# RWKV attention and a token mixer in one kernel: V in its loaded rows, scores by token parity, the bonus summed in PSUM

## The chip, the cores and the metric

The kernel runs on one core of a Trainium2 chip. The metric is device time in microseconds (us), the median of several runs. Five units take part: TensorE (PE) multiplies and writes only to PSUM, the accumulator memory; VectorE (DVE) and ScalarE (ACT) do elementwise work and are the ones that carry results out of PSUM; GpSimd (POOL) works between SBUF tensors here; SyncE (SP) issues the DMA transfers.

## The reference

Shapes: batch B = 4, heads H = 8, tokens S = 768, head width D = 48; the model width is H x D = 384.

```python
for t in range(S):
    cur = einsum('bhd,bhe->bhde', u * k[t], v[t])
    y[t] = einsum('bhd,bhde->bhe', r[t], state + cur)
    state = w[t][..., None] * state + einsum('bhd,bhe->bhde', k[t], v[t])
x = y.transpose(0, 2, 1, 3).reshape(B, S, 384)
wq, wk = x @ w_q, x @ w_k                        # 384 -> 64
W = einsum('bsd,btd->bst', wq, wk) / 8           # tokens by tokens, no softmax
out = maximum(einsum('bst,btd->bsd', W, x), 0) @ w_out
```

The first part is a linear recurrence with a decay w for each channel and token, and a bonus u for the current token. The second mixes all 768 tokens of a batch. All inputs and outputs are float32 in HBM.

## The kernel before

**Units.** The work is cut into 12 units, three of 256 tokens for each batch. A unit is two chunks of 128 tokens, called c = 0 and 1. A load puts two neighbouring tokens of all heads into one partition: partitions 0 to 63 hold chunk 0, the others chunk 1, and j = 0 or 1 is the token's parity. From unit 1 on, k and r are loaded with four tokens to a partition row (`load_long`, L237), and the V of the last batch is loaded at once in four scattered pieces (`load_whole`, L243).

**The recurrence as matrix products.** For each unit ScalarE takes the logarithm of w (`ln`, tile lw). TensorE sums the logarithms over the tokens with a triangle of ones (`cw`), and ScalarE turns the sums into `ep` (exponential) and `en` (exponential of the negative). A constant MU is added to each logarithm ("centring", SHIFT), and the factors gx, gv, gk, US and IDU take it out again. TensorE transposes k and r (`kT`, `rT`) with a permutation PM, so that channels lie on partitions. Elementwise products then give RT = r ep (step `RT`, L516), KT = k en (`KT`, L521 and L526) and qT = r k for the bonus (`qT`, L506); `ks` is a copy of the turned k in SBUF.

- Scores: `A` multiplies KT by RT for each head and chunk, 128 tokens by 128, and `AM` (L595) multiplies by the causal mask US on VectorE.
- V: `v16` casts it to bf16, `vp` multiplies by PM to bring its rows into the chunk order, and `VB` copies that out of PSUM.
- State: `kb` turns KT back, `kd` copies it out with the factor gk, `sn` multiplies it by VB and adds the old state through IDU, and `SB` multiplies by the decay.
- Output: `yi` is RT times the old state and `ya` is AM times VB, both summed in PSUM in tile y. The even and odd heads lie in separate banks of y, except in the last unit.
- Bonus: `dps` sums qT times u, `dd` copies the sums out, `Vd` (L575) multiplies them by VB on GpSimd, and `X` (L710, L715) computes y gx + Vd on VectorE, into X in bf16.

**The mixer.** `xt` and `XT` turn X, `qk` gives both projections, `QK` copies them out. After the third unit of a batch, `T` sums wk times X over all tokens, `TS` copies it out, and for each unit `mx`, `rl` (relu), `fp` (times w_out), `os` (copy) and `st` (store) finish.

**What sets the order.** Nothing is scheduled at run time. `add` collects steps with their key, the engines they may run on, and what they come after. WAYS picks an engine for each step that has a choice (E or e or c TensorE, D or d VectorE, A ScalarE, P GpSimd), BANKS places the PSUM tiles in the eight banks, and ORDER is the written order in which all steps are issued. Each engine runs its own steps strictly in that order and waits by semaphores. `RINGS` says how many buffers each tile has: four for the loaded tensors, two for most others. All transfers but two of u and one store are issued on SP's queue in its order. The steps `z` are products of zeros that keep TensorE busy.

The instructions of TensorE all carry the line of the helper `mm`, L179; the copies those of `copy`, L327 to L335.

```python
s["eng"] = self.ENGINE[s["way"]]
...
for i in ORDER:
    s = self.steps[i]
    assert all(x["out"] for x in s["after"]), s["key"]
```

Of the kernel before, what the change touches and what calls it, by code (L numbers as in the profile page):

```python
# [12 lines left out]
I32 = mybir.dt.int32  # L13
# [10 lines left out]
class Buf:  # L24
    def __init__(self, kind, tile=None):
        self.kind = kind
        self.tile = tile
        self.filler = None
        self.before = None
        self.bank = None  # L30


class Plan:

    ENGINE = dict(E="E", e="E", c="E", A="A", D="D", d="D", P="P", S="S", Q="Q", L="L")
# [5 lines left out]
    def add(self, key, ways, fn, after=(), buf=None, reads=(), cols=0, mode=0, behind=None,  # L43
            half=-1, more=None):
        s = dict(key=key, ways=ways, way=ways[0], fn=fn, after=list(after), buf=buf,
                 reads=list(reads), cols=cols, mode=mode, behind=behind, half=half,
                 more=more or {}, i=len(self.steps), fills=False, out=False)
        if buf is not None:
            if buf.filler is None:
                buf.filler = s  # L50
                s["fills"] = True
                if buf.tile is None:
                    self.banks.append(buf)
                elif behind is None and buf.before is not None:
                    s["behind"] = buf.before.filler
            elif behind is None:
                s["behind"] = buf.filler
        self.steps.append(s)
        return s

    def order(self):
        ways = iter(WAYS)
        for s in self.steps:
            if len(s["ways"]) > 1:
                s["way"] = next(ways)
                assert s["way"] in s["ways"], s["key"]
            s["eng"] = self.ENGINE[s["way"]]
        for b, x in zip(self.banks, BANKS):
            b.bank = x
        assert sorted(ORDER) == list(range(len(self.steps)))  # L70
        done = []
        for i in ORDER:
            s = self.steps[i]
            assert all(x["out"] for x in s["after"]), s["key"]
            if s["buf"] is not None and s["buf"].kind == "x":
                s["buf"].kind = "s" if s["way"] == "E" else "w"
            s["out"] = True
            done.append(s)
        return done


ORDER = [
# [40 lines left out]
]  # L123
WAYS = (
    "PDDDAPPDDdPADPPDDEEEAAPPAdPAAPEAcEEAAPPAPPADPeDEEDAAAAAAAAPPDPDADPeAcEEDAPPAdPAAPEAEEEDA"
    "PPDPPAAPeAEEAAAAAAAAAAPDPPAAPEDEcEAAPPDPPDAPEAEEEAAPPDPPAAPeDceAAAAADADDPAAPPAPEDcEEDAPP"
    "DPPAPeAcceAAPPDPPPAPPAEEDDAEDADAAADAAAADADDA"
)
BANKS = [
# [9 lines left out]
WARM = 12  # L139
# [3 lines left out]
def kernel(  # L143
# [27 lines left out]
    LONG = tuple(range(1, N))  # L171
    WHOLE = (B - 1,)

    SHIFT = 25
    MU = -SHIFT * math.log(2.0) / C
    UNIT = 2.0 ** -SHIFT

# [9 lines left out]
    def const(shape, dtype, name):  # L187
# [3 lines left out]
    EW = 136  # L191
    KW = 64 + 16 * 128
# [5 lines left out]
        kd=(2, KW, BF16), lw=(2, 1024, BF16), r16=(2, 1024, BF16), k16=(2, 1024, BF16),  # L198
        ep=(2, 8 * EW, BF16), en=(2, 1024, BF16), ks=(2, 1024, BF16), qT=(2, 1024, BF16),
        RT=(2, 1024, BF16), KT=(2, 1024, BF16), v16=(2, 2 * DM, BF16), VB=(2, 2 * DM, BF16),  # L200
        dd=(2, 2 * H, F32), Vd=(2, 2 * DM, BF16), AM0=(2, 1024, BF16), AM1=(2, 1024, BF16),
        SB=(4, NP * D, BF16), XT=(2, 2 * DM, BF16), MX=(4, 2 * DM, BF16), X=(2, NCH * DM, BF16),
        QK=(2, QW, BF16), TS=(2, DM, BF16), vw=(2, NCH * DM, F32))
    if not WHOLE:
        del RINGS["vw"]
# [14 lines left out]
    PM = const([C, C], BF16, "PM")  # L220
    IDU = const([C, C], BF16, "IDU")
    Z = const([C, 512], BF16, "Z")
    US = const([C, C], F32, "US")
# [24 lines left out]
    def setup():  # L248
        pads = [[64, 16], [1, 16]]
        nc.vector.memset(Z, 0.0)  # L250
        for _ in range(18):
            mm(PS[:, ds(0, 512)], Z[:, ds(0, C)], Z)
# [641 lines left out]
```

## Time and profile before

| | |
|---|---|
| time, median of 3 runs | 102.12 us (101.38 to 103.38) |
| the profiled execution's own time | 101.37 us |
| its span | 99.6 us |
| PE busy | 86.6 us, 1906 matmuls |
| VectorE busy | 84.9 us, 154 instructions |
| ScalarE busy | 79.0 us, 135 instructions |
| GpSimd busy | 69.5 us, 82 instructions |
| HBM read, written | 19.66 MB, 4.72 MB |
| granted TensorE clock | 1.0 |

The profile is of one execution. The span goes from its first to its last instruction. A group's row gives the busy time of its instructions together, the mean of one in ns, and the idle time of the engine just before them with what ended it. In a timeline, a row is a run of like instructions: its start, how long it lasted, and how many. Neighbouring instructions of one engine overlap somewhat, and a matmul's end is modelled, so the distance from one start to the next says more than the length. PE's busy time counts overlapping matmuls once.

### The profile page before, as it was taken

The page shows a single profiled execution, that of the slowest core. Times are in us where ns is not written, and L with a number is a line of the kernel's source. Part 1 is how long each engine was busy: PE and PEld are TensorE (multiplying, and loading weights), DVE is VectorE, ACT ScalarE, POOL GpSimd, SP SyncE. Part 2 cuts the span into 40 slices and gives each one's busy share as a digit, 9 for nine tenths or more (in the row PEclk, how much of TensorE's full clock was granted, in tenths as well). Part 3 has the DMA queues.
Part 4 walks back from the last instruction along what each step waited for, and adds up shares of the span by engine and source line. Part 5 has one row for each costly group of instructions (what it writes and reads, how often), then busy time and mean ns, then how long its engine had stood idle before and what let it go on. Part 6 is the DMA issues. An engine that isn't in the chain of part 4 may idle for free.

```text
span 99.6 us, 4492 instructions
## 1 busy us (share of the span) xinstructions
PE 86.6 (87%) x1906; PEld 63.3 (64%) x1911; DVE 84.9 (85%) x154; ACT 79.0 (79%) x135; POOL 69.5 (70%) x82
## 2 busy tenths in 40 slices
PE   5978796879886998999999999889998999999930
PEld 1325473756774767777776777759787687776610
DVE  6284999799979999979999999999999799783740
ACT  6034998799996799899999998999899766666920
POOL 6866354999799895799999989498996392500000
PEclk9999999999999999999999999999999999999999
DMA  1999999799999999999999977998993056030794
GB/s 17 313 327 349 324 337 296 195 295 335 289 314 298 225 311 329 344 321 268 271 330 305 316 114 218 251 156 201 282 417 115 7 210 264 10 158 7 277 367 149
DMA packets 45141, 24.68 MB, mean 248 GB/s; under 512 B 31552, under 2 KB 43968, under 8 KB 45120
## 3 DMA queue, kind: packets, MB, share of 16 engines
q1 hardware_dynamic: 44960, 24.19, 84.0%
q8 instruction: 15, 0.25, 0.9%
q10 hardware_dynamic: 160, 0.20, 0.5%
q14 instruction: 6, 0.05, 0.1%
HBM read 19.66 MB, written 4.72 MB: 245 GB/s over the span
## 4 chain that ended last, share of the span: by engine, by line
PE 37%; DVE 23%; SPq 20%; DMA 7%; issue 7%; ACT 3%; ACTq 0%; DVEq 0%
PE PS L179 37%; SPq L232 9%; SPq L237 8%; DMA vg<-in_v_dram 7%; DVE AM L595 7%; DVE X L710 6%; DVE RT L516 3%; SPq L355 2%; DVE qT L506 2%; DVE ks L333 2%; DVE SB L658 1%; ACT VB L327 1%; SPq L357 1%; ACT MX L339 1%; DVE kd L335 1%
## 5 line engine op out<-in xcount | busy, mean ns | idle before, releaser
L595 DVE TENSOR_TENSOR AM<-PS,US 128x1024 bf16<-128x1024 f32 x24 | 28.8, 1218 | 0.7 <-PE PS L179 0.7
L526 POOL TENSOR_TENSOR KT<-ks,en 128x1024 bf16<-128x1024 bf16 (+1 forms) x10 | 19.7, 1965 | 4.7 <-DVE ks L333 3.3
L575 POOL TENSOR_TENSOR Vd<-VB,dd 128x768 bf16<-128x768 bf16 (+1 forms) x14 | 18.1, 1293 | 4.5 <-ACT dd L327 3.4
L454 ACT ACTIVATE en<-PS 128x1024 bf16<-128x1024 f32 (+1 forms) x14 | 12.5, 907 | 3.0 <-PE PS L179 2.9
L179 PEld LDWEIGHTS <-KT 48*128 48x128 bf16 (+1 forms) x312 | 9.7, 94 | 6.6 <-issue 4.5
L447 ACT ACTIVATE ep<-PS 128x512 bf16<-128x512 f32 (+1 forms) x28 | 13.7, 555 | 0.1
L179 PE MATMUL PS<-wo,MX 128*128 128x384 bf16 x72 | 13.5, 327 | 0.0
L710 DVE SCALAR_TENSOR_TENSOR X<-PS,gx,Vd 128x384 bf16<-128x384 f32 x22 | 12.5, 609 | 0.7 <-PE PS L179 0.6
L407 ACT ACTIVATE lw<-wg 128x768 bf16<-128x768 f32 x12 | 10.3, 857 | 2.9 <-DMA wg<-in_w_dram 2.9
L179 PE MATMUL PS<-RT,KT 48*128 48x128 bf16 x192 | 9.7, 218 | 1.2 <-ACT VB L327 0.4
L327 ACT COPY os<-PS 128x768 f32<-128x768 f32 (+1 forms) x11 | 7.9, 714 | 3.5 <-PE PS L179 3.5
L418 POOL CAST k<-kg 128x768 bf16<-128x768 f32 x10 | 8.3, 827 | 2.5 <-DMA kg<-in_k_dram 2.5
L179 PE MATMUL PS<-Z 128*128 128x512 bf16 x25 | 8.4, 461 | 1.4 <-DVE Z L250 1.2
L418 POOL CAST r<-rg 128x768 bf16<-128x768 f32 x10 | 8.2, 825 | 1.6 <-DMA rg<-in_r_dram 1.6
L179 PEld LDWEIGHTS <-MX 128*128 128x128 bf16 x72 | 6.5, 97 | 3.6 <-DVE MX L341 0.2
L516 DVE TENSOR_TENSOR RT<-PS,ep 128x1024 bf16<-128x1024 bf16 (+1 forms) x14 | 8.4, 605 | 0.0
L179 PE MATMUL PS<-VB,AM 128*128 128x48 bf16 x192 | 8.0, 184 | 0.4 <-issue 0.4
L506 DVE TENSOR_TENSOR qT<-PS,ks 128x1024 bf16<-128x1024 bf16 x12 | 8.2, 684 | 0.1
L339 ACT ACTIVATE MX<-PS 128x768 bf16<-128x768 f32 (+1 forms) x12 | 8.0, 682 | 0.4
L179 PE MATMUL PS<-CM,lw 64*128 64x128 bf16 x192 | 7.4, 217 | 0.5 <-DVE AM L595 0.3
L327 ACT CAST VB<-PS 128x768 bf16<-128x768 f32 x8 | 6.4, 804 | 1.1 <-PE PS L179 0.6
L179 PEld LDWEIGHTS <-AM 128*128 128x128 bf16 x192 | 6.3, 96 | 1.6 <-issue 0.7
(90 smaller groups left out, 191.9 us busy)
## 6 DMA issues: line engine op xcount, KB each, us to landing
kg<-in_k_dram SPq DMA_DIRECT2D x12, 384.0 KB, 6.4
wg<-in_w_dram SPq DMA_DIRECT2D x12, 384.0 KB, 5.0
rg<-in_r_dram SPq DMA_DIRECT2D x12, 384.0 KB, 5.8
vg<-in_v_dram SPq DMA_DIRECT2D x9, 384.0 KB, 6.3
out_dram<-os SPq DMA_DIRECT2D x9, 384.0 KB, 2.5
vw<-in_v_dram SPq DMA_DIRECT2D x4, 288.0 KB, 6.7
out_dram<-os SPq DMA_DIRECT2D x5, 192.0 KB, 2.4
wof<-in_moe_w_out_dram SPq DMA_DIRECT2D x1, 576.0 KB, 6.2
```

Source lines behind the costliest of these rows:

```text
L179: return nc.tensor.matmul(o, l, rr, start=start, stop=stop, skip_group_check=True, is_transpose=trans)
L327: nc.scalar.copy(o, i)
L407: nc.scalar.activation(view(lw.tile, 0, [[64, H], [512, 2], [1, D]]), view(g["wg"].tile, 0, [[D2, H], [D, 2], [1, D]]), ACT.Ln, bias=0.0, ...
L418: op(view(o.tile, 0, [[64, NP], [256, 4], [1, D]]), view(g[src].tile, 0, [[2 * D2, NP], [D, 4], [1, D]]))
L447: nc.scalar.activation(view(ep.tile, cs[0] * NP * EW + off, [[EW, NP * len(cs)], [step, 2], [1, 32]]), view(at(cw), cs[0] * 512 + j * 64, ...
L454: nc.scalar.activation(en.tile[:, ds(cs[0] * 512, w_)], at(cw)[:, ds(cs[0] * 512, w_)], ACT.Exp, bias=0.0, scale=-1.0)
L506: lambda e: nc.vector.tensor_tensor(plain(qT.tile), turned(512), plain(ks.tile), ALU.mult),
L516: nc.vector.tensor_tensor(plain(RT.tile, cs, 32), turned(512, cs, True), plain(ep.tile, cs, EW // 4), ALU.mult)
L526: x.tensor_tensor(KT.tile[:, cols], ks.tile[:, cols], en.tile[:, cols], ALU.mult)
L575: (nc.vector if e == "D" else nc.gpsimd).tensor_tensor(Vd.tile[:, cols], VB.tile[:, cols], view(dd.tile, cs[0] * H, [[1, len(cs) * H], [0, ...
L595: AMs[c] = add(("AM", n, c), "D", lambda e, c=c, A=A: nc.vector.tensor_tensor(view(AM[c].tile, 0, [[C, 8], [1, C]]), view(at(A), 0, [[C, 8 ...
L710: nc.vector.scalar_tensor_tensor(view(X.tile, 2 * i * DM + hh * D, [[D2, H], [1, D]]), view(at(y), hh * 512, [[D, H], [1, D]]), gx, view(V ...
```

## The change

- V stays in its loaded rows of two tokens: `vp` and `VB`, the permutation PM and `load_whole` go; `v16` (three buffers) is what all products read. k and r are loaded in two-token rows too; `load_long` goes.
- No centring: MU, gx, gv, gk, UNIT and IDU go. `kd` is a plain copy.
- Scores by the parity j of the key token, on tiles of 64 rows by 64 columns. A step `A` has 16 products in place of 8, and its mask is US[j]. `ya` sums over j and over chunk halves: 16 products of 64 rows in place of 8 of 128.
- State: `sp` is the products of kd and v16 on 64x64 tiles, `so` adds the old state through ID16.
- The bonus is added in PSUM: `yd` multiplies Vd by the identity into y, and `X` is a plain copy of y on ScalarE or VectorE.
- All heads of a chunk now lie in one bank of y. `yi` is in two steps, one for each pairing of chunk and half of the partitions. Where both kinds of rows would meet in y, order() sets a drain of TensorE before the step (20 places).
- `kb` and `xt` are always on tiles of 64 rows. `ep` is one activation in place of two, and `ep` and `RT` aren't halved in the first and last unit.
- New ORDER, WAYS and BANKS; 8 z steps in place of 12, 16 products of zeros at the start in place of 18. By the new WAYS, X runs on ScalarE but for one half, KT mostly on VectorE (GpSimd keeps 6 pieces of KT out of 10, and 10 of Vd out of 14), and XT, QK and dd more often on VectorE.

```diff
+            if s["rows"] is not None:
+                x, kind = s["rows"]
+                s["drain"] = x.rows.get(1 - kind) == drains
+                drains += s["drain"]
+                x.rows[kind] = drains
...
-    v16=(2, 2 * DM, BF16), VB=(2, 2 * DM, BF16), ... vw=(2, NCH * DM, F32)
+    v16=(3, 2 * DM, BF16)
...
+        def f_ep(e):
+            nc.scalar.activation(view(ep.tile, 66, [[EW, 8], [-65, 2], [1, 64]]),
+                                 view(at(cw), 0, [[C, 8], [64, 2], [1, 64]]), ACT.Exp)
...
             def f_A(e, j=j, A=A):
                 for hp in range(NP):
-                    for hh in range(2):
-                        mm(x[:, ds(hh * 512 + hp * C, C)],
-                           KT.tile[ds(hh * 64, D), ds((c * NP + hp) * C, C)],
-                           RT.tile[ds(hh * 64, D), ds((c * NP + hp) * C, C)])
+                    for c in range(2):
+                        for hh in range(2):
+                            mm(x[ds(c * 64, 64), ds(hh * 512 + hp * C, C)],
+                               KT.tile[ds(hh * 64, D), ds((2 * hp + j) * C + c * 64, 64)],
+                               RT.tile[ds(hh * 64, D), ds((c * NP + hp) * C, C)])
...
+                        for c in chunks:
+                            mm(at(sn[c])[ds(hh * 64, 64), ds(hp * D, D)],
+                               kd.tile[ds(c * 64, 64), ds((j * H + h) * 64, 64)],
+                               v16.tile[ds(c * 64, 64), ds(j * DM + h * D, D)],
+                               start=(j == 0 and hp == 0), stop=True)
...
+        for hx in range(2):
+            halves = [(c, c ^ hx) for c in range(2) if olds[c] is not None]
+            def f_yi(e, hx=hx, halves=halves):
+                for hp in range(NP):
+                    for c, hh in halves:
+                        mm(of(c, 2 * hp + hh), RT.tile[ds(hh * 64, D), ds((c * NP + hp) * C, C)],
+                           olds[c].tile[ds(hh * 64, D), ds(hp * D, D)],
+                           start=y.begin(c), stop=False)
...
+                    for c in range(2):
+                        mm(of(c, h), AM[j].tile[ds(c * 64, 64), ds((hh * NP + hp) * C, C)],
+                           v16.tile[ds(c * 64, 64), ds(j * DM + h * D, D)],
+                           start=y.begin(c), stop=True)
...
+        def f_yd(e):
+            first = [y.begin(c) for c in range(2)]
+            for j in range(2):
+                for c in range(2):
+                    mm(at(y)[ds(j * 64, 64), ds(c * 512, DM)], ID16[ds(c * 64, 64), ds(c * 64, 64)],
+                       Vd.tile[ds(c * 64, 64), ds(j * DM, DM)], start=first[c])
...
-                    nc.vector.scalar_tensor_tensor(
-                        view(X.tile, 2 * i * DM + hh * D, [[D2, H], [1, D]]),
-                        view(at(y), hh * 512, [[D, H], [1, D]]), gx,
-                        view(Vd.tile, hh * D, [[D2, H], [1, D]]), ALU.mult, ALU.add)
+            xs = add(("X", n, c0), "AD", lambda e, c0=c0, nc_=nc_: copy(
+                e, view(X.tile, (2 * i + c0) * DM, [[DM, nc_], [1, DM]]),
+                view(at(y), c0 * 512, [[512, nc_], [1, DM]])),
+                yss, [X], [(y, sum(1 << c for c in cs))], cols=DM * nc_)
...
         for s in plan.order():
+            if s["drain"]:
+                nc.tensor.drain()
```

More of the change, by code (lines that the diff above doesn't have):

```diff
@@ L41, in __init__, with add @@
         self.banks = []
[L43 to L57, printed above, removed]
+    def add(self, key, ways, fn, after=(), writes=(), reads=(), cols=0, mode=0, more=None,
+            rows=None):
+        full = lambda x: x if isinstance(x, tuple) else (x, 3)
+        s = dict(key=key, ways=ways, way=ways[0], fn=fn, after=list(after),
+                 writes=[full(x) for x in writes], reads=[full(x) for x in reads], cols=cols,
+                 mode=mode, more=more or {}, i=len(self.steps), out=False, drain=False, rows=rows)
+        for x, _ in s["writes"]:
+            if x.banks and x not in self.banks:
+                self.banks.append(x)
         self.steps.append(s)
@@ new lines, in spread @@
+        def spread(t, place, pitch, js):
+            if len(js) == 2:
+                return view(t, place, [[64, 8], [pitch, 2], [1, 64]])
+            return view(t, place + js[0] * 64, [[C, 4], [pitch, 2], [1, 64]])
+        ens, KTs = {}, {}
+        for js in fine:
+            x = add(("en", n, js[0]), "A", lambda e, js=js: nc.scalar.activation(
+                packed(en.tile, js), spread(at(cw), 0, 512, js), ACT.Exp, scale=-1.0),
+                [cws], [en], [cw], cols=512 * len(js))
+            for j in js:
+                ens[j] = x
@@ L562, in f_dps @@
             x = at(dps)
-            for c in range(2):
+            for j in range(2):
                 for hp in range(NP):
-                    mm(x[:, ds(c * H + hp * 2, 2)], qT.tile[:, ds((c * NP + hp) * C, C)],
-                       view(UB, hp, [[NP, 2]]), start=(c == 0 and hp == 0), stop=True)
-        dpss = add(("dps", n), "E", f_dps, [qTs, wts["u"]], dps, [qT])
+                    mm(x[:, ds(j * H + hp * 2, 2)], qT.tile[:, ds((2 * hp + j) * C, C)],
+                       view(UB, hp, [[NP, 2]]), start=(j == 0 and hp == 0), stop=True)
@@ L627, in unit @@
-        olds, oldss = [], []
-        for c in range(2):
-            old = batch.get("SB")
-            olds.append(old)
-            oldss.append(batch.get("SBs"))
-            if final and c == 1:
-                break
-            sn, SB = bank(), ring("SB")
-            def f_sn(e, c=c, old=old, sn=sn):
-                x = at(sn)
-                for o in range(2 if e == "c" else 1) if old is not None else ():
-                    rows = ds(o * 64, 64) if e == "c" else ds(0, 128)
-                    mm(x[rows, ds(0, NP * D)], IDU[:, rows], old.tile, start=True, stop=False)
+                    for c in range(2):
[3 more added lines that the diff above has]
+                               RT.tile[ds(hh * 64, D), ds((c * NP + hp) * C, C)])
@@ L641, in f_sn, with f_sp @@
+        chunks = [0] if final else [0, 1]
+        sn = [bank() for _ in chunks]
+        olds, oldss = [batch.get("SB")], [batch.get("SBs")]
+        def f_sp(e):
+            for j in range(2):
                 for hp in range(NP):
@@ L661, in unit @@
-                [sns, eps[c]], SB, [sn, ep])
-        ys = [bank(), bank()] if end else [wide()] * 2
-        yis, yas = {}, {}
-        def of(c, h):
-            return at(ys[c])[:, ds(h * D if end else h % 2 * 512 + (c * NP + h // 2) * D, D)]
-        def f_yi(e, c, start):
-            heads = [(hp, hh) for hp in range(NP) for hh in range(2)]
-            if end:
-                heads.sort(key=lambda x: x[1])
-            for x, (hp, hh) in enumerate(heads):
-                if end and x == NP:
-                    nc.tensor.drain()
-                mm(of(c, 2 * hp + hh), RT.tile[ds(hh * 64, D), ds((c * NP + hp) * C, C)],
-                   olds[c].tile[ds(hh * 64, D), ds(hp * D, D)],
-                   start=(start and hp == 0 and not (end and hh)), stop=False)
@@ L697, in unit @@
-        for c in range(2):
-            if c not in yas:
-                y_add(c)
+                ("SB", n, c), "D", lambda e, c=c, SB=SB: nc.vector.tensor_tensor(
+                    view(SB.tile, 0, [[D, NP], [1, D]]), view(at(sn[c]), 0, [[D, NP], [1, D]]),
+                    view(ep.tile, c * NP * EW + 64, [[EW, NP], [0, D]]), ALU.mult),
+                [x, eps], [SB], [sn[c], ep])
+            olds.append(SB)
+            oldss.append(batch["SBs"])
+        y = wide()
+        def of(c, h):
+            return at(y)[:, ds(c * 512 + h * D, D)]
```

472 lines of the change are left out of this document (163 added, 309 removed), and 92 rows, old and new, of tables (BANKS, ORDER).

## The prediction

> **What bounds the kernel now.** First the page: busy shares, the slices, the chain.
>
> ```profile
> span 99.6 us, 4492 instructions
> PE 86.6 (87%) x1906; PEld 63.3 (64%) x1911; DVE 84.9 (85%) x154; ACT 79.0 (79%) x135; POOL 69.5 (70%) x82
> ...
> PE   5978796879886998999999999889998999999930
> ...
> DVE  6284999799979999979999999999999799783740
> ...
> PE 37%; DVE 23%; SPq 20%; DMA 7%; issue 7%; ACT 3%; ACTq 0%; DVEq 0%
> ```
>
> The chain has three stretches: loads at first, VectorE in the middle, TensorE at the end. PE's digits overstate it, since a pipelined matmul counts until its modelled end, so I check with busy time by stretch and then with the timeline.
>
> ```profile
> 30.00:40.00 10.00, 8.70 (x235) 6.69 (x232) 10.00 (x17) 8.36 (x14) 8.39 (x8) 1.00 1.02 293
> ...
> 50.00:60.00 10.00, 9.64 (x233) 7.38 (x227) 10.00 (x17) 9.93 (x18) 9.46 (x9) 1.00 0.96 260
> 60.00:70.00 10.00, 9.42 (x276) 7.47 (x274) 10.00 (x17) 9.64 (x16) 8.24 (x7) 1.00 1.00 214
> ```
>
> After the length come the busy times of PE, weight loads, DVE, ACT and POOL; then the clock (full), the DMA share, GB/s. VectorE has no gap in 30 of these us, ScalarE hardly one. The loads run at 0.96 to 1.02 of the DMA engines, so they aren't idle either. VectorE's own timeline, first and last piece of its stretch:
>
> ```profile
> 8.52 0.69 DVE L333 COPY ks<-PS 128x1024 bf16<-128x1024 bf16 x1 [0.94 <-PE PS L179]
> ...
> 83.23 2.34 DVE L595 TENSOR_TENSOR AM<-PS,US 128x1024 bf16<-128x1024 f32 x2
> ```
>
> From 8.52 to 85.57 VectorE is paced by little but itself; after the last score mask AM, TensorE and the final token mixing take over. Two AM take 2.34, though one alone reads 1.218 below, so a VectorE instruction costs its mean less about 0.08; I use that throughout.
>
> ```profile
> L595 DVE TENSOR_TENSOR AM<-PS,US 128x1024 bf16<-128x1024 f32 x24 | 28.8, 1218 | 0.7 <-PE PS L179 0.7
> L710 DVE SCALAR_TENSOR_TENSOR X<-PS,gx,Vd 128x384 bf16<-128x384 f32 x22 | 12.5, 609 | 0.7 <-PE PS L179 0.6
> ...
> L333 DVE COPY ks<-PS 128x1024 bf16<-128x1024 bf16 x8 | 5.5, 685 | 1.7 <-PE PS L179 1.7
> L333 DVE COPY XT<-PS 128x768 bf16<-128x768 bf16 x4 | 2.2, 550 | 0.0
> ...
> L333 DVE COPY os<-PS 128x384 f32<-128x384 f32 x3 | 1.6, 549 | 0.0
> L521 DVE TENSOR_TENSOR KT<-PS,en 128x1024 bf16<-128x1024 bf16 x2 | 1.4, 678 | 0.0
> L333 DVE CAST v<-vg 128x768 bf16<-128x768 f32 x1 | 1.3, 1306 | 0.7 <-DMA vg<-in_v_dram 0.7
> ...
> L333 DVE CAST VB<-PS 128x768 bf16<-128x768 f32 x1 | 0.9, 949 | 0.0
> ```
>
> **VectorE, term by term, up to the last AM.** The counts come from the diff's WAYS and ORDER, read as each engine's list. Removed: X's 22 half-tile adds (units 0 to 10), 22 x 0.53 = 11.7. Three ks copies fewer (8 to 5), 1.8. VB of unit 7, 0.9. RT no longer halved in the first and last unit, and one SB now behind the mask, 0.5. Together 14.9. Added, because the diff's lists hand VectorE other work instead: KT straight out of PSUM, six at 0.60 and one from SBUF (no such full-size row; 0.6 to 2.1, I take 1.2) against two and a bit before, 3.0. Four more XT, 1.9. Four QK copies (384 columns, the os row's 0.47), 1.9. Two Vd from SBUF (bounded by 0.6 as the KT row and 1.48 as POOL's; I take 1.0 as 768 elements lie between), 2.0. One cast of r or v more, 1.2. One relu, 0.9, which I price as the VB row, as wide. Seven dd, three quarters of a kd and UB, 1.0. Together 11.9. **Net -2.9**, bounds -4.0 to -1.0 from the two SBUF forms. AM's 24 stay; the mask becomes two tiles of the same form. The short runs of 64 in KT and qT I take at no cost: X's operands are runs of 48 today, and a run-length cost would add at most a few tenths.
>
> **ScalarE and GpSimd.**
>
> ```profile
> L447 ACT ACTIVATE ep<-PS 128x512 bf16<-128x512 f32 x20 | 11.0, 611 | 0.0
> ...
> L454 ACT ACTIVATE en<-PS 128x1024 bf16<-128x1024 f32 x10 | 10.3, 1028 | 0.3 <-PE PS L179 0.2
> L327 ACT CAST VB<-PS 128x768 bf16<-128x768 f32 x8 | 6.4, 804 | 1.1 <-PE PS L179 0.6 <-issue 0.4
> ```
> ```profile
> L526 POOL TENSOR_TENSOR KT<-ks,en 128x1024 bf16<-128x1024 bf16 x8 | 17.4, 2169 | 2.3 <-ACT ep L447 1.1 <-DVE ks L333 0.8 <-ACT en L454 0.3
> L575 POOL TENSOR_TENSOR Vd<-VB,dd 128x768 bf16<-128x768 bf16 x10 | 14.8, 1478 | 1.8 <-ACT dd L327 1.4 <-DMA vg<-in_v_dram 0.3
> ```
>
> ScalarE loses eight VB (6.4), some of ep (two pieces of 0.61 become one like en's 1.03, 2 us over twelve units), five XT of VB's width and five QK of half of it (4 and 2), and gains eleven full X copies of VB's size (0.80 each, 8.8) and a half, three ks of about en's price (3.1) and some output copies: about -3 to -4 in all, more before the last unit. Being nearly full beside VectorE, it must fall too for VectorE's gain to show, and it does. GpSimd loses six KT pieces (four full, at 2.17) and four Vd; it ends 10 us lighter and paces nothing.
>
> **TensorE pays.** Busy time is no use for prices, so I take start to next start from its timeline.
>
> ```profile
> 60.55 0.36 PE L179 MATMUL PS<-v,PM 64*64 64x384 bf16 x4
> 60.84 0.39 PE L179 MATMUL PS<-Z 128*128 128x512 bf16 x1
> ...
> 79.70 0.28 PE L179 MATMUL PS<-VB,kd 128*64 128x48 bf16 x8
> 79.92 0.37 PE L179 MATMUL PS<-SB,RT 48*128 48x48 bf16 x16
> 80.13 0.26 PE L179 MATMUL PS<-ID,KT 48*128 48x48 bf16 x8
> ...
> 82.75 0.62 PE L179 MATMUL PS<-RT,KT 48*128 48x128 bf16 x16
> 83.21 0.60 PE L179 MATMUL PS<-SB,RT 48*128 48x48 bf16 x8
> 83.75 0.35 PE L179 MATMUL PS<-UB,qT 128*128 128x2 bf16 x8
> 83.96 1.14 PE L179 MATMUL PS<-wo,MX 128*128 128x384 bf16 x6
> 85.03 0.35 PE L179 MATMUL PS<-ID,X 64*128 64x64 bf16 x12
> ...
> 85.76 0.57 PE L179 MATMUL PS<-VB,AM 128*128 128x48 bf16 x16
> 86.17 0.49 PE L179 MATMUL PS<-QK,TS 128*128 128x256 bf16 x3
> ...
> 93.45 2.11 PE L179 MATMUL PS<-wo,MX 128*128 128x384 bf16 x12
> ```
>
> - Scores: 16 in 0.46, 29 ns each, two row groups at once. On 64x64 tiles there are 384 instead of 192. Four v,PM of 384 columns took at most 0.29 to the next start, though one 384-column matmul alone is about 163 ns (12 in 2.11 less the last one's tail), so four tiles do run together. A quarter of the 58 ns that one takes is 14.5: nothing added; by v,PM's 0.29 scaled to 128 columns it is 24 ns, +3.6. I take +0.7.
> - Values (ya): 16 in 0.41, 26 ns each, on the whole array. The new 384 use 64 rows each, two at once, as the SB,RT products did, 16 in 0.21 or 13 ns: no change.
> - States: 20 steps of 0.29 become 320 products at 13 ns and 16 small additions, -0.3. V's permutation (nine of 0.29) goes and the bonus product yd (twelve of the same form) comes, +0.9. All kb and xt now on 64-row tiles, cheaper, -1.7; other, +0.2.
> - Drains: products from two row groups now meet in one bank of y, and the order puts an explicit drain at 20 places. The eight SB,RT at 83.21 contain one today: 0.54 to the next start, where eight take 0.11, so 0.3 to 0.4 each. 20 instead of 2, **+5.9**.
> - Changes of tile shape between neighbouring steps: 109 after 103 (0.09 each, from the six wo,MX that should end at 84.94 and the next start at 85.03), +0.5.
>
> **Sum +6.2**, bounds +4 to +11. Can TensorE take it? By such prices its steps need 5.5 us a unit, 66 in twelve, and 103 changes 9: some 76 of the 87 us from 8.5 to 95.56 (the last wo,MX). It has about 11 free, 3 of them at the start, where it waits for loads anyway. +6.2 fits, with less slack; I charge 0.3 for the longer waits of engines that now go more evenly. The tail from the first score of the last unit (82.75) to 95.56 loses one drain, one dps and one mx and gains sp, yd, so and xt of unit 9: within 0.1.
>
> By the Trainium skill (TensorE: Matmul & The Clock Gate, "Wait — 56ns, not 53.3ns?") starts never follow each other in under about 25 ns. The SB,RT row's 13 ns over two row groups differs from that, so here the measurement decides; were it 25 for every matmul, it would be the rival of small matmuls below, about 107 by its price.
>
> **Loads.** 768-byte pieces of k and r become 384-byte ones, and the last batch's V comes in rows too.
>
> ```profile
> 10.00:20.00 10.00, 7.86 (x212) 5.74 (x213) 9.26 (x18) 9.11 (x18) 5.63 (x7) 1.00 1.04 287
> ...
> HBM read 19.66 MB, written 4.72 MB: 245 GB/s over the span
> ```
> ```profile
> 67.87 1.69 SPq L237 DMA_DIRECT2D rg<-in_r_dram  x1
> ```
> ```profile
> 74.04 0.83 POOL L418 CAST k<-kg 128x768 bf16<-128x768 f32 x1
> ```
>
> 19.66 MB at the 287 to 293 GB/s of the stretches without the odd V form is 67 to 69 us. The last load is issued from 67.87 to 69.56, k's of that unit before it, and the last k is cast only at 74.04: some us of slack. V's four scattered loads made the 214 GB/s stretch; they go. I take 0; bounds -1 to +2. On SP's queue vg and kg of the last unit stand behind the first store; its copy is early in ScalarE's order, so it shouldn't hold them.
>
> **Total.** -2.9 + 0.3 + 0 = -2.6: span 97.0. The profiled execution took 101.37, 1.77 beside its span, so 98.8; that execution lies 0.75 under the median of 102.12, and I put the forecast a little up, at **99.1** (about 3% under the median).
>
> **Rivals.**
> 1. ScalarE's larger relief sets the pace, and the tail shortens with it: another -3, **96**. For it: ACT 9.93 of 10 at 50 to 60. Against: VectorE was full longer.
> 2. TensorE becomes the bound: drains at 0.43 and scores at the upper price, 6.2 + 1.7 + 2.9 = 10.8, past the 8 us that are truly free, and VectorE's gain is lost in waits: 98.8 + 2.7 = **101.5**. For it: 9.4 to 9.6 in the late stretches. Against: much of that is modelled ends.
> 3. Small matmuls don't overlap beyond today's forms (the tiles do not do what is meant): 192 more scores at 29 ns, 192 ya at 26, 160 state products at the 27 ns of VB,kd (eight in 0.22) are 5.6 + 5.0 + 4.3 = 14.9 on top of 5.9 for drains, 20.8 or so. It decides once TensorE gets more than 8; 12.8 over, less about half that falls where VectorE waits today: 99.6 + 6 + 1.77, about **107**, slower. Against: the 13 ns of SB,RT and v,PM's 0.29.
> 4. The loads set the pace: all at 260 GB/s, 75.6 us for 19.66 MB, against the 71 at which k would be needed; less what V's form cost, +2: **100.9**.
>
> **Chances.** Forecast 0.50 (its own range 96.5 to 100.8), rivals in order 0.08, 0.19, 0.15, 0.08. Over 2%, about what a measurement of this kernel can tell from no change, means under 100.1: 0.42 of the forecast, all of rival 1, 0.05 of 2 and 4 give 0.55. Within: 0.08 + 0.10 + 0.05 = 0.23. Over 104.2: the rest of 2 and 3, 0.22. The range 95.5 to 104.5 leaves out rival 3 and a twentieth below.
>
> **What would show it.** Right: X rows gone from VectorE and at 0.80 on ScalarE; VectorE's last AM ends near 83 with no gap of over 1 us in the middle; score groups of 16 start within 0.25 of the next; last wo,MX ends near 93. Wrong: VectorE with gaps released by PE, 16 ya at over 0.3 a group, drained groups of 0.6 and more, or casts of k waiting for DMA after 60 us.

## The result, and the profile after

The changed kernel takes 119.88 us (118.06 to 120.73, four runs) against 102.11 of the kernel before (101.38 to 103.38): a ratio of 1.166, 95% interval 1.146 to 1.185. Executions of one kernel differ by some per cent, the slower ones mostly at a lower granted clock; the ratio is of the faster ones alone (119.42 and 118.06 here), and the profiled one is among the slower. The forecast was 99.1, with a range that ended at 104.5. The profiled execution took 120.73 us, 1.7 beside its span.

The page after, its shares, slices, instruction queue and chain (lines and columns as in the page before):

```profile
span 119.0 us, 5806 instructions
PE 97.9 (82%) x2588; PEld 70.1 (59%) x2588; DVE 80.3 (67%) x144; ACT 78.3 (66%) x107; POOL 55.8 (47%) x65
...
PE   5954976899489866996989895699999779999993
...
DVE  6025988657295893572898788379899888876520
...
PEclk9999555555555996799999999869999999999999
...
q8 instruction: 20, 0.33, 1.2%
...
PE 61%; DVE 14%; ACT 13%; issue 10%; DVEq 0%; ACTq 0%
```

Two lines of the page before, not shown with the prediction:

```profile
PEclk9999999999999999999999999999999999999999
...
q8 instruction: 15, 0.25, 0.9%
```

VectorE is 4.6 us less busy than before, ScalarE 0.7 and GpSimd 13.7, and the kernel is 17.8 us slower. TensorE is busy for 11.3 us more, part of it at half clock, but for 82% of the span instead of 87%: all engines stand more. Two lines changed that the prediction did not look at. TensorE's granted clock (PEclk, in tenths of full speed), full throughout before, is at half in nine slices and partly in others. And the queue that brings TensorE's instructions moved 20 packets instead of 15.

The prices of the single steps came out about as forecast. Groups on the other engines, and two stretches of TensorE's timeline:

```profile
L277 ACT CAST X<-PS 128x768 bf16<-128x768 f32 (+1 forms) x12 | 9.3, 777 | 8.2 <-PE PS L170 8.2
...
L446 DVE TENSOR_TENSOR KT<-PS,en 128x1024 bf16<-128x1024 bf16 (+1 forms) x7 | 4.6, 651 | 4.0 <-PE PS L170 2.6 <-ACT en L400 0.9 <-ACT ks L277 0.4
L283 DVE COPY ks<-PS 128x1024 bf16<-128x1024 bf16 x5 | 3.4, 690 | 6.2 <-PE PS L170 6.1
```
```profile
54.32 0.37 PE L170 MATMUL PS<-v,AM 64*128 64x48 bf16 x16
54.62 0.35 PE L170 MATMUL PS<-Vd,ID 64*64 64x384 bf16 x2
56.04 0.35 PE L170 MATMUL PS<-Vd,ID 64*64 64x384 bf16 x2 [1.07 <-issue]
...
59.91 0.42 PE L170 MATMUL PS<-RT,KT 48*64 48x128 bf16 x16 [0.34 <-DVE RT L438]
60.26 0.37 PE L170 MATMUL PS<-ID,KT 48*128 48x48 bf16 x16
```

Sixteen values take 0.30 to the next start, sixteen scores 0.35, with a change of shape behind them. But the third row shows what a sum of products cannot: a step of four products stops after two, for 1.42 us from start to start, and waits for nothing that the profile knows. I call such a pause a stand. There are more, also in the middle of steps:

```profile
43.53 0.28 PE L170 MATMUL PS<-wk,XT 128*128 128x64 bf16 x4
45.53 0.29 PE L170 MATMUL PS<-wk,XT 128*128 128x64 bf16 x2 [1.72 <-issue]
...
73.58 0.40 PE L170 MATMUL PS<-v,kd 64*64 64x48 bf16 x26 [0.44 <-ACT X L277]
75.37 0.24 PE L170 MATMUL PS<-v,kd 64*64 64x48 bf16 x6 [1.40 <-issue]
...
96.55 0.28 PE L170 MATMUL PS<-RT,KT 48*64 48x128 bf16 x8
97.61 0.31 PE L170 MATMUL PS<-RT,KT 48*64 48x128 bf16 x8 [0.79 <-issue]
```

Cut the trace at the ends of these stands, and the windows count TensorE's products (PE) and weight loads (PEld) between them:

```profile
45.50:55.95 10.45, 8.99 (x254) 6.84 (x254) 5.62 (x10) 6.29 (x9) 5.84 (x7) 0.84 0.99 260
55.95:75.30 19.35, 15.86 (x510) 11.77 (x511) 15.10 (x23) 16.31 (x21) 8.73 (x8) 1.00 0.94 253
75.30:97.55 22.25, 20.23 (x638) 14.82 (x637) 18.44 (x31) 16.07 (x23) 16.29 (x14) 0.92 0.25 88
```

That is 508, 1021 and 1275 instructions; with the few drains and semaphore instructions in between these are 512, 1024 and 1280, or 2, 4 and 5 times 256. TensorE's instructions come in blocks of 256, 0.33 MB in 20 packets or 16.5 KB each, and where the next block is late, TensorE stands. In these windows a block takes 5.2, 4.8 and 4.5 us on average. The Trainium skill (Runtime: NRT & Kernel Launch, "Instruction fetch mechanics") describes this refill in 16 KiB blocks of 256 instructions and calls the crossing mostly hidden; the spacing agrees, "hidden" does not hold here.

I add up, over a trace, the gap from start to start at each 256th instruction, less 0.06 us; a few hold another wait too. The kernel before gives 2.4 us for 15 blocks, the changed one 6.8 for 20. By the same count the blocks that came late in the changed kernel came 5.6, 4.8 and 5.1 us after the one before, and 4.0 once the loads were done. So the stands that can be seen grew by 4.4 of the 17.8 us.

### The profile page after: what moved, and what is told of

Read it like the earlier page. It is cut to its first block, busy times and chain, and to the rows that moved or that the text cites. A ratio compares the mean times of both kernels' runs of the same rounds, so it can differ in the third digit from the quotient of the medians.

```text
span 119.0 us, 5806 instructions
## 1 busy us (share of the span) xinstructions
PE 97.9 (82%) x2588; PEld 70.1 (59%) x2588; DVE 80.3 (67%) x144; ACT 78.3 (66%) x107; POOL 55.8 (47%) x65
## 4 chain that ended last, share of the span: by engine, by line
PE 61%; DVE 14%; ACT 13%; issue 10%; DVEq 0%; ACTq 0%
PE PS L170 61%; DVE AM L487 6%; ACT ks L277 4%; DVE KT L446 3%; DVE RT L438 2%; ACT X L277 2%; ACT MX L289 2%; ACT kd L277 2%; ACT en L400 1%; ACT ep L383 1%; DVE SB L534 1%; ACT lw L347 1%; DVE MX L291 0%; DVE kd L283 0%; DVE Vd L468 0%
## 5 line engine op out<-in xcount | busy, mean ns | idle before, releaser
L468 POOL TENSOR_TENSOR Vd<-v,dd 128x768 bf16<-128x768 bf16 x10 | 14.8, 1477 | 29.2 <-DVE dd L283 20.4
L170 PEld LDWEIGHTS <-KT 48*64 48x64 bf16 (+1 forms) x576 | 12.7, 117 | 7.0 <-issue 5.2
L277 ACT CAST X<-PS 128x768 bf16<-128x768 f32 (+1 forms) x12 | 9.3, 777 | 8.2 <-PE PS L170 8.2
L383 ACT ACTIVATE ep<-PS 128x1024 bf16<-128x1024 f32 x12 | 12.5, 1044 | 3.2 <-PE PS L170 2.7
L170 PE MATMUL PS<-RT,KT 48*64 48x128 bf16 x384 | 11.4, 253 | 3.2 <-DVE RT L438 1.7
L170 PE MATMUL PS<-wo,MX 128*128 128x384 bf16 x72 | 13.1, 327 | 0.1
L446 POOL TENSOR_TENSOR KT<-ks,en 128x512 bf16<-128x512 bf16 (+1 forms) x6 | 9.8, 1639 | 4.7 <-ACT ks L277 3.1
L277 ACT COPY ks<-PS 128x1024 bf16<-128x1024 bf16 x7 | 7.1, 1012 | 7.3 <-PE PS L170 4.2
L347 ACT ACTIVATE lw<-wg 128x768 bf16<-128x768 f32 x12 | 10.2, 847 | 2.1 <-DMA wg<-in_w_dram 2.1
L438 DVE TENSOR_TENSOR RT<-PS,ep 128x1024 bf16<-128x1024 bf16 x12 | 8.2, 688 | 4.7 <-PE PS L170 3.9
L170 PE MATMUL PS<-v,AM 64*128 64x48 bf16 x384 | 9.9, 191 | 0.5
L357 POOL CAST v<-vg 128x768 bf16<-128x768 f32 x11 | 9.0, 825 | 0.4 <-DMA vg<-in_v_dram 0.4
```

The source lines that it names most:

```text
L170: return nc.tensor.matmul(o, l, rr, start=start, stop=stop, skip_group_check=True, is_transpose=trans)
L277: nc.scalar.copy(o, i)
L347: nc.scalar.activation(view(lw.tile, 0, [[64, H], [512, 2], [1, D]]), view(g["wg"].tile, 0, [[D2, H], [D, 2], [1, D]]), ACT.Ln)
L357: op(view(o.tile, 0, [[D, H], [DM, 2], [1, D]]), view(g[src].tile, 0, [[D2, H], [D, 2], [1, D]]))
L383: nc.scalar.activation(view(ep.tile, 66, [[EW, 8], [-65, 2], [1, 64]]), view(at(cw), 0, [[C, 8], [64, 2], [1, 64]]), ACT.Exp)
L438: nc.vector.tensor_tensor(view(RT.tile, 0, [[512, 2], [64, 8], [1, 64]]), view(at(kr, BF16), 512, [[1024, 2], [64, 8], [1, 64]]), view(ep. ...
```

## The experiments

The kernel before was measured beside each of them, with medians of 101.45 to 102.30 us. Times are medians, with the lowest and the highest behind them. "Stands at block ends" are sums by the count above. Where a kernel has a new order, the edit is in the lists ORDER, BANKS and WAYS alone.

**First guess: the clock, the zeros, the drains, the loads.**

e1, 20 early zero products in the changed kernel (8 at the end before):

```diff
-WARM = 8
+WARM = 20    # ORDER: ahead of kT, cw, rT, A, kb of units 0 to 2
```


> The changed kernel with 20 products of zeros put between TensorE's steps of the first three units (8 stood at the very end). Clock theory: the granted clock stays at 1.0 in the first 40 us instead of falling to 0.5 at 12 us; the span falls from 119 to 100 to 105 and the mean clock is over 0.97. Work theory (drains and more, smaller products make TensorE the bound at any clock): the clock may rise, but the span stays over 112, with TensorE still named in the waits of VectorE and ScalarE.

119.18 us (117.21 to 122.00). The half-clock time of the profiled run fell from 34.1 to 17.1 us, the median by 0.7. So the early clock is not most of it.

e2, the kernel before with its 12 zeros at the end of ORDER:

> The kernel before with its 12 products of zeros all moved to the end of TensorE's list. Clock theory: the granted clock falls to 0.5 between 10 and 20 us here too and the time rises by 5 to 15 us over 102.1. Work theory: the time stays within 2 us of 102.1, since the zeros are no work that anyone waits for; the clock may fall briefly and come back, as TensorE has slack here.

103.62, ratio 1.019 (1.012 to 1.027). Its trace is at half clock from 10.7 to 21.0: 10 us at half clock, with all that came of them, cost 1.9.

e3, drains in the kernel before:

```diff
             if end:
                 heads.sort(key=lambda x: x[1])
+            else:
+                nc.tensor.drain()
```


> The kernel before with a drain of TensorE ahead of each of its 18 yi steps outside the last unit (it has 2 drains, the changed kernel 20). My price of 0.3 to 0.4 each: TensorE has some 8 us free, so 5 to 7 us of drains cost the time 0 to 2 us. Work theory: 4 to 7 us, nearly the whole price, since TensorE has no real slack. Clock theory: the time moves less than 2 us unless the clock falls under 0.97.

103.71 against 101.69, ratio 1.018 (1.011 to 1.025): 18 drains cost 2.0 us. That is the price that reached the time; on TensorE they cost more. Two yi steps and the step behind them, before, then in e3 with a drain between the two:

```profile
43.96 0.36 PE L179 MATMUL PS<-SB,RT 48*128 48x48 bf16 x16
44.26 0.35 PE L179 MATMUL PS<-UB,qT 128*128 128x2 bf16 x8
...
45.20 0.63 PE L179 MATMUL PS<-SB,RT 48*128 48x48 bf16 x16
45.76 0.35 PE L179 MATMUL PS<-UB,qT 128*128 128x2 bf16 x8
```

From the last product ahead of a yi step to its first there are 0.29 us in median in e3 and 0.10 before: about 0.2 for a drain, some 3.5 us for 18, where 0.3 to 0.4 each were forecast. Over half of that reached the time.

e4, e1 without the loads of k, r and v from unit 4 on:

```diff
+            few = name != "wg" and n > 3
-            g[name + "L"] = dma((name, n), lambda e, ap=ap, ...
+            g[name + "L"] = dma((name, n), None if few else lambda e, ap=ap, ...
```


> The kernel of the first run, but k, r and v are not loaded after the fourth unit (each unit then works on the data of four units before), which takes 24 of 48 loads away. If TensorE's idle pieces of 0.8 to 1.7 us that wait for nothing shown are its instruction stream held up by the loads, they go and the span falls 3 to 6 us below the first run's. If they are something of TensorE's own, they stay and the span is within 1.5 us of the first run's. If the loads pace the changed kernel, POOL's waits for DMA go and the span falls too, but the pieces stay.

115.59 (114.64 to 116.53), 3.6 less than e1; stands at block ends 4.4 us instead of 5.9. The time falls as was expected if the loads hold up TensorE's instructions, but the stands become fewer and do not go. Most of the 17.8 us stays.

**Second guess: the written order.** Theory 1 says that the written order makes the engines wait on one another, theory 2 that the work is too long in any order. A search replayed each engine's queue with the trace's durations and moved steps.

e5, order and banks new, engines kept:

> The changed kernel with its zero products early (119.2 us), every step on the same engine as there, only the order in which the steps are issued and the PSUM banks they get are new: an order found by a search that replays each engine's queue with the durations that the trace showed. No instruction is added, removed or resized. Theory 1 (the work sums were right, and the written order makes TensorE, VectorE and ScalarE wait on one another: 35.2 us of TensorE's waits against 22.0 before): half or more of the 13 us comes back, 109 to 114 us. Theory 2 (the work itself is too long, or TensorE's instructions come too late, whatever the order): 117 to 121 us, as without the new order.

e6, KT and Vd free to change engine:

> As the last, with an order of its own, and the products KT and Vd may change engine: four more KT and two more Vd go to GpSimd (2.12 and 1.48 us each there, against 0.69 and 1.17 on VectorE), two KT of half size come back from it. Theory 1, sharpened (the change also emptied GpSimd, 82 to 56 us, onto VectorE, and the waits sit in VectorE's queue): 3 us less than the order alone, 106 to 111 us. If the engines of KT and Vd do not matter: the same as the order alone within 1.5 us.

e7, all engines free:

> As the last, but every step that may run on several engines was free to change engine in the search: eight more os copies on VectorE, XT, QK and dd partly on ScalarE, the copies ks on VectorE. Same instructions in number and size, but for the engine. Theory 1: near the kernel before, 102 to 107 us, since the work sums forecast 99 and TensorE's drains and the instruction gaps stay. Theory 2: above 113 us.

136.34 (134.15 to 142.06), 133.50 (132.39 to 135.16) and 127.90 us (123.98 to 130.32), far over every expectation, with TensorE at half clock for 41 to 55 us of the profiled runs. These three say nothing on the theory, since the new lists also reordered the loads, and the replay let data land before its turn on the queue. The waits of e5:

```profile
POOL v L355 <- DMA vg<-in_v_dram: 8.5, 1, 8.5
POOL k L358 <- DMA kg<-in_k_dram: 4.7, 1, 4.7
```

e8, the loads at their real pace, engines free, 24 zero products:

> The changed kernel with a second plan of its own: order, PSUM banks and engines from the search, in which the loads now keep the pace that the traces show (1.25 us each on one queue, 3.4 us to land), and with 24 zero products put where TensorE would stand in the first 45 us. No instruction is added, removed or resized but the zero products. Theory 1 (the work is not too long; the written plan makes three engines that are each busy some 75 to 80 us wait on one another): 103 to 109 us against 119 for the changed kernel. Theory 2 (TensorE's 682 more products, their instructions and drains set the time whatever the plan): above 114 us.

e9, the same with the changed kernel's engines and order of loads:

> As the last, but every step stays on the engine that the changed kernel gives it and the loads keep its order; only the order of the steps on TensorE, VectorE, ScalarE and GpSimd, the PSUM banks and the 24 zero products are new. Theory 1: 109 to 114 us, that is, about half of what the whole plan brings comes from the order alone and half from the engines. Theory 2: 117 to 121 us. If only the engines matter: 117 or more as well, but with the run before well below it.

120.49 (115.95 to 122.42) and 125.11 (119.70 to 127.20), both over what theory 1 gave. In e8's trace TensorE's gaps that VectorE and ScalarE released are fewer (13.3 us against 20.6 in the changed kernel, from one product's start to the next), yet the stands at block ends are 9.8 us instead of 6.8. The block ends took part of what the better order gave. The replay still had the loads land too early, after 3.4 us; in the changed kernel's trace it is 5.7 in median from an issue's start and 4.4 from its end.

**Third: the instruction supply.**

Theory 3 says that TensorE's instructions, in blocks of 256, come too late. Its rival says that only TensorE's time and the waits count.

e10 and e11, in the kernel before, behind the scores of each of the 24 A steps. Both add products into the scores' banks and change the scores.

```diff
+                for q in range(28):                             # e10
+                    hh, o = q % 2, q // 2 % 2
+                    mm(x[ds(o * 64, 64), ds(hh * 512, 8)], Z[ds(hh * 64, 64), ds(0, 64)],
+                       Z[ds(hh * 64, 64), ds(0, 8)], start=False)
+                for q, w_ in ((0, 512), (1, 384)):              # e11
+                    mm(x[:, ds(q * 512, w_)], Z[:, ds(0, C)], Z[:, ds(0, w_)], start=False)
```


> The kernel before, with 28 small products of zeros (64x64 tile, 8 columns) behind the scores in each of the 24 A steps: 672 products or 1344 TensorE instructions more, 3825 to 5169, nearly the changed kernel's 5205, and some 13 ns each, 8.7 us of TensorE's time in all. Theory 3 (TensorE's instructions come in blocks of 256, since the traces show its unexplained stands at instructions 958 + 256k and nowhere else, and a block takes 4 to 6 us to come while the loads run): 109 to 116 us, and at least 4 us over the kernel with the same TensorE time in 48 large products. Rival (only TensorE's time and the waits count): the same as that kernel within 1 us.

> The kernel before, with two large products of zeros (512 and 384 columns, 0.37 us together) behind the scores in each of the 24 A steps: 8.9 us of TensorE's time, as in the run with small products, but 96 instructions more instead of 1344. Theory 3 and its rival both: 104 to 108 us, the price of TensorE's time on the way from scores to VectorE; the distance to the run with small products tells them apart.

e11: 108.42, ratio 1.064 (1.057 to 1.072). e10: 120.63, ratio 1.179 (1.167 to 1.190): 12.2 us more, over the 109 to 116 that theory 3 gave, and as slow as the changed kernel, though nothing of V, order or drains was touched. TensorE does not spend longer on the small products: from the first added one to the next step's first there are 0.32 us in median in e10, and 0.39 to 0.49 in e11. The page of e10 first, then of e11:

```profile
PE 105.5 (90%) x2578; PEld 77.3 (66%) x2583; DVE 88.1 (75%) x154; ACT 79.9 (68%) x135; POOL 69.7 (59%) x82
...
PEclk9999855557999555579999999999999999999997
...
q8 instruction: 20, 0.33, 1.2%
```
```profile
PE 94.5 (89%) x1941; PEld 66.0 (62%) x1959; DVE 85.9 (80%) x154; ACT 79.5 (75%) x135; POOL 69.6 (65%) x82
...
PEclk9999999999999999999999999999999999999999
...
q8 instruction: 15, 0.25, 1.0%
```

Stands at block ends are 5.0 us in e10 and 1.5 in e11; e10 also lost its clock for 28.6 us, e11 never. So many small products do both things; this pair does not part them. e11 says something else too: some 9 us of added products (24 pairs of 0.39 us), with 96 more instructions, cost 6.5 us (108.42 against 101.87).

e12, e1 with half as many products in three kinds of step (here the states). It leaves out the second chunk's scores and the odd heads' states and score columns, and other data takes their place:

```diff
-                    for hh in range(2):
-                        h = 2 * hp + hh
-                        for c in chunks:
-                            mm(at(sn[c])[ds(hh * 64, 64), ds(hp * D, D)],
-                               kd.tile[ds(c * 64, 64), ds((j * H + h) * 64, 64)],
+                    for c in chunks:
+                        mm(at(sn[c])[:, ds(hp * D, D)],
+                           kd.tile[ds(c * 64, 64), ds((j * H + 2 * hp) * 64, 128)],
...
```


> The changed kernel with its zero products early (119.2 us), where the scores, the states and the products of the scores with V take half as many products of twice the width: the second chunk's scores, odd heads' states and odd heads' score columns are left out (other data takes their place), 544 products or 1088 TensorE instructions fewer. Steps, order, drains, and every instruction of the other engines stay, and TensorE streams as many columns. Theory 3: 108 to 113 us, the stands at block ends fall from 5.9 to about 2.5 us and the half-clock stretches behind them go. Rival (waits of the written order, drains): 116 to 120 us.

e13, the same edit in e8:

> The changed kernel's second plan (120.5 us, with 9.8 us of stands at block ends in its profile), with the same halved products and what they leave out. Theory 3: 104 to 110 us, since that plan waits less on VectorE and ScalarE (13.3 us of TensorE's gaps against 16.6) and lost it all at block ends. Rival: 116 to 121 us.

113.41 (110.12 to 114.89) and 112.84 (110.73 to 116.17), 5.8 and 7.7 us less than e1 and e8, with every step of the other engines as it was. Both lie just above what theory 3 gave (to 113 and to 110) and well below its rival; e12 was at half clock for 24 us of its profiled run. Not all of the gain need be the supply: products of twice the width take TensorE somewhat less time as well. By the median spacing of starts in e14 and e16 below, a product of AM and v goes from 12.9 to 20.6 ns and one of the states from 11.7 to 13.1, at half the number; with the scores that is some 2.8 us over the kernel.

**The clock and the supply together.**

Theory 4 says that the clock falls when little of TensorE's array works, and that zero products over the whole array bring it back.

e14, 38 zero products in the changed kernel:

> The changed kernel with 38 zero products (128x128 tile, 512 columns, 0.21 us each) instead of 8: the 20 early ones and 18 more where its trace shows TensorE waiting over 0.35 us, up to 102 us. Theory 4 (the granted clock goes to half when little of the array works in 3.4 us: the full tile counts whole, a 64x64 tile a quarter; in all traces a drop followed a stretch with 0.14 to 0.44 of the array at work, whatever share of the time TensorE was busy): mean clock 0.95 or more against 0.887 in the run with 20, and 113 to 117 us, since runs of one kernel differ by some 60 us for a whole clock. Rival (the clock only follows the waits, and costs little): the clock may rise, the time stays at 118 to 122, or rises with the 3.9 us of added products.

e15, 36 zero products in e13:

> The second plan with halved products (112.8 us; it leaves out and replaces the same products) with 36 zero products instead of 24, the 12 more where its trace shows TensorE waiting over 0.35 us. Theory 4: mean clock 0.97 or more against 0.93 and 109 to 112 us. Rival: 112 to 115 us.

e14: 120.09 (117.52 to 121.68). The clock came back (0.955 in the profile, half clock 10.8 us), the time did not: theory 4 was wrong in its number. The waits of e14, and one of its stands:

```profile
PEld L170 <- issue: 29.3, 80, 1.9
...
PE PS L170 <- issue: 6.6, 8, 1.8
```
```profile
68.04 0.30 PE L170 MATMUL PS<-ID,X 64*128 64x64 bf16 x7
70.17 0.23 PE L170 MATMUL PS<-ID,X 64*128 64x64 bf16 x3 [1.82 <-issue]
```

Its stands at block ends sum to 9.5 us. TensorE at full clock runs through a block sooner and stands longer for the next; but the 18 zero products more than in e1 are also 3.9 us of work, and e14 does not part the two. e15: 111.54 (110.59 to 114.00), 1.3 less than e13.

e16, e14 with the halved products:

> The changed kernel in its written order with both remedies: the 38 zero products of the last run (120.1 us, mean clock 0.95, 9.5 us of stands at block ends) and the halved products (113.4 us with 20 zero products, mean clock 0.91; it leaves out and replaces the same products). Theory 3 with 4 (the instruction supply binds first, and the clock only counts once it does not): 109 to 112 us, stands at block ends under 4 us. If the two simply add, the zeros bring nothing or cost their 4 us here as they did there: 113 to 117 us. If the halving only helped by chance of the clock: 117 or more.

110.48 (110.19 to 113.92), ratio 1.090 (1.083 to 1.097), 9.6 us less than e14 for 1088 instructions fewer. Its clock and waits:

```profile
PEclk9999997599999999999999999999999999999999
```
```profile
PEld L170 <- issue: 22.7, 77, 1.0
```

Stands at block ends are 2.5 us, as in the kernel before, and half clock 3.4 us. With e1 (119.18), e14 (120.09) and e12 (113.41) this makes a square. By medians the added zero products bring nothing (-0.9) while the instructions are many, and 2.9 when they are fewer; fewer instructions bring 5.8 and 9.6. By the lowest times (117.21, 117.52, 110.12 and, for e16, 110.19) the zeros bring nothing in either case, and fewer instructions 7.1 and 7.3. At nearly the same granted clock, 0.966 and 0.961, an execution of e14 took 117.52 us and one of e12 110.12. So that fewer, wider products help is shown, apart from the clock. That the clock counts only once they are fewer is not shown; e12 alone scatters from 110.12 to 114.89. No version with the change beats the kernel before.

## Why the prediction was wrong, step by step

- **VectorE's net -2.9** (its terms give -3.0): right in kind and nearly in size. X's rows are on ScalarE at 0.80, KT from PSUM at 0.69, and VectorE is 4.6 us less busy over the span. It no longer decides anything. Its last AM ends at 105.23 instead of 85.57 (forecast: near 83), with gaps that TensorE releases, which was the first of my signs for "wrong":

```profile
102.88 2.35 DVE L487 TENSOR_TENSOR AM<-PS,US 128x1024 bf16<-128x1024 f32 x2
```

- **ScalarE -3 to -4**: it fell by 0.7. **GpSimd -10**: 13.7. Neither matters.
- **TensorE's products**: right. At full clock sixteen values take 0.20 to 0.31 to the next start where 0.21 was forecast, sixteen scores 0.25 to 0.35 where 0.25 was; rival 3, whose small matmuls do not overlap, is refuted. The **drains** at 5.9 were priced too high: at about 0.2 each (e3), 18 are some 3.5 us of TensorE's time.
- **The step that failed: "It has about 11 free ... +6.2 fits, with less slack; I charge 0.3."** Two things failed in it. The first is the charge: in e11, some 9 us of large products behind the scores, on the way to VectorE, cost 6.5 us, so the free time was not where the work was added. At that share, 0.7, the forecast's own 6.2 would have cost 4 to 5 us and not 0.3, an estimate from e11. The second is what the sum left out: the room was worked out from the time of products and shape changes alone, not from how many instructions TensorE has to get. Some 680 products more with their weight loads are about 1360 instructions, five blocks and a third; e10 shows such a number, in no more TensorE time than e11's large products, to cost 12.2 us more. The counts were in view, x1906 on the page and the products in the diff, and the trace before already had four stands of 0.4 to 0.7 us at block ends. I read the weight loads' waits for "issue" as noise; before first, then after:

```profile
PEld L179 <- issue: 14.8, 52, 0.7
```
```profile
PEld L170 <- issue: 29.3, 81, 1.8
```

  At the 4.0 to 5.6 us of a late block, 20.3 blocks are 81 to 114 us, my estimate, before the first wait for another engine; 15 are 60 to 84. It is a rough one, since a block can also pass in 3.6 us (85.0 to 88.6 of the changed kernel, the loads done). That is no sum with 11 us of slack in it.
- **The 0.3 for longer waits**: the supply and the clock together are worth at most 119.9 - 110.5 = 9.4 us, by e16, which keeps the order and the drains but whose products also take less time. The other 9.0 that e16 lies over the kernel before (101.45 beside it) are not undone by any run. In e16's trace TensorE's gaps released by VectorE are 13.1 us against 8.5 before, from one product's start to the next, and those with a drain 3.4 against 0.2, 7.8 more together; this is read from the trace, and how much of it is the new order stays open, since e8 and e9 changed the order while the supply was binding.
- **Rivals**: rival 2, TensorE becomes the bound, is the nearest in kind; at 101.5 it was far too cheap, because its price was dearer drains and slower scores, neither of which came. Its mechanism was another. Rival 1 did not come either: ScalarE was hardly relieved, and the tail is no shorter.
- **The tail** "within 0.1" holds: from the end of the last AM to the last wo,MX there were 10.0 us before and are 10.0 after (105.23 to 115.25).

```profile
112.15 3.10 PE L170 MATMUL PS<-wo,MX 128*128 128x384 bf16 x18
```

- **Loads 0**: no cast of k waits for its load after 60 us. GpSimd waits 8.3 us for one v there, and half of the loads taken out (e4) bring 3.6 us, part of it as shorter stands; so the loads cost a little more than nothing, and not only as data.

## What to carry to other kernels

Before a change that splits products into smaller ones, count TensorE's instructions, two for each product, as well as their time: here a late block of 256 took 4.0 to 5.6 us, and a gain elsewhere can be eaten at the block ends. A gap of TensorE in the middle of a step, with "issue" as its releaser, is the sign; count the instructions between two of them. A remedy that leaves the time where it was (the clock in e14) is not yet refuted as a cause: look whether another wait has grown by as much, or whether the remedy itself costs what it gives.

## What the hardware showed that I had not expected

- Every stand of over 0.55 us inside a step, in any trace here, lies within eight instructions of number 958 + 256k, counted along TensorE's recorded instructions; the longest took 3.1 us (e13).
- TensorE's half-clock stretches, where the end of the run does not cut them, are 3.4 us or a multiple (27.3 us in the changed kernel, 10.2 in e2). Two of the changed kernel:

```profile
45.50:48.90 3.40, 3.37 (x85) 2.99 (x86) 1.39 (x3) 1.49 (x3) 0.00 (x0) 0.51 1.05 288
...
76.30:79.70 3.40, 3.40 (x68) 2.06 (x61) 2.38 (x5) 1.89 (x3) 2.90 (x3) 0.50 0.29 109
```

  The first begins where a stand ends, the second 0.9 us behind one. The Trainium skill (TensorE: Matmul & The Clock Gate, "Part 1: The HAM clock gate (the "warmup" mystery)") gives the window of 3.4 us and the half rate, and the trace agrees. What counts as activity stays open. Weighing each product by its rows and columns, the 3.4 us ahead of a drop had 0.14 to 0.44 of the array at work, while products kept TensorE busy for up to 0.83 of them (e10); e10 and e11 fit that (0.88 and 1.0 of the clock at the same added time). But the kernel before, which kept its clock, has such stretches down to about 0.3, so the measure does not part the two cases, and no run changed it by itself.
